# Attention and two feed-forward layers on one core: adjacent heads as pairs, keys on 128 partitions, another order of the first loads

## The chip, the cores and the metric

The kernel runs on one core of a Trainium2 chip. The metric is the device time of one execution in microseconds (us); lower is better. Five engines run side by side: TensorE (PE), VectorE (DVE), ScalarE (ACT), GpSimd (POOL) and SyncE (SP). Each takes its instructions in order. SP only issues DMA transfers; ACT and POOL can issue them too, between their own instructions. SPq, ACTq and POOLq are the places where such an issue shows.

## What is computed

Eight batches of 8 heads, 576 queries, head size 64. Keys and values are first averaged over groups of 8 positions, which leaves 72 of each; the scores, a softmax and the product with the averaged values follow. The result, 4608 rows of 512, passes through two feed-forward layers. The weights are float64 and are turned into float32 in the kernel.

```python
k_p = k.reshape(B, H, 72, 8, D).mean(axis=3)      # v_p likewise
scores = scale * np.matmul(q, k_p.transpose(0, 1, 3, 2))
attn = softmax(scores);  x = matmul(attn, v_p)    # (8, 8, 576, 64) -> (4608, 512)
h = x @ w_in;  x = (h * cos(h)) @ w_out           # 512 -> 2048 -> 512
out = (silu(x @ w_gate) * (x @ w_val)) @ w_out2   # 512 -> 1536 -> 512
```

## The kernel before

**Stages.** First comes an opening part for batch 0 of the attention; then 144 slots, each one 512-row block of tokens times one 128-column block of the first feed-forward layer (9 blocks of rows, 16 of columns); then the second layer. The attention of batches 1 to 7 is spread over the slots, by the tables MID, LATE, EXP and NORM and the first slot of each batch in START (lines 377 to 423).

**Heads.** The 8 heads are worked on as 4 pairs; before, pair p is heads p and p + 4 (`"(r p)"` in the views of q, k and v). The two heads of a pair share the 128 partitions.

**Queries.** `load_q` brings a batch in as four transfers, each of 32 partitions in runs of 32 numbers (128 bytes), so that 32x32 blocks lie ready, and `do_qt` turns each tile of queries with DVE's block transpose. There are five tiles, four of 128 queries and one of 64. `ACT_QUEUE` lists which transfers are issued by ACT: half of batch 0, and all of batches 1 and 3. The others are issued by SP.

**Keys and values.** A raw key tile has 72 partitions, one for each group of 8 positions; three additions (`pool_sum`) sum the 8. Values put the first 64 groups of two heads on 128 partitions, and the last 8 groups of all heads in one more tile. Batch 0 is summed on DVE from `kst` and `vst`, batch 1 on DVE from tiles that borrow the homes of late w_in tiles (`load_kv1`, homes wa3* and wa2*). Batches 2 to 7 are loaded by SP (`load_kv`) and summed on POOL, 8 key tiles and 5 value tiles per batch, one per slot (`do_raw`). `prep_k` turns the sums with TensorE and writes them scaled to `kT`.

**Scores.** `do_s` multiplies, takes the extreme with DVE, and for batches 0 and 1 ACT takes one exponential per head. `do_norm`, `do_pt` and `do_av` follow, and the result goes to `ring`. `x_split` cuts `ring` into a high and a low part, `xhl`.

**Weights.** The 16 tiles of w_in and 16 of w_out, 512 KB each, are turned from float64 by the generator `conv`: on DVE `cv_exp` (L445), `cv_sign` (L456), `cv_high` (L462), `cv_low` (L467) and `cv_mul` (L473), on ACT `cv_bias` (L451); for w_in also a split (L974 on ACT, L987 on DVE). `order` begins with 8 tiles of w_in, and then tiles of w_out and of w_in take turns. `fill(m)` advances the generator by m steps. `load_i(m)` issues the next m loads of w_in, `load_o(m)` those of w_out, which have two buffers. In the first 16 slots there is one `load_i` per slot.

**Order.** The opening part is the string `program`: s, x, p, a are scores, softmax, turn and product of a tile; V, K, U sum values of batch 0, keys and values of batch 1; v and k prepare; f and F advance the conversion; i, o, q load; w makes room for w_out; X is `x_split`. The framework then orders the instructions of each engine by its own planner, so what stands later in the text can be issued earlier.

Of the kernel before, what the change touches and what calls it, by code (L numbers as in the profile page):

```python
# [25 lines left out]
def fused_kernel(  # L26
# [18 lines left out]
    nc = tc.nc  # L45
# [22 lines left out]
    Y32 = NF1  # L68
    ACT_QUEUE = {(0, 0), (3, 1), (1, 1), (3, 0), (1, 0)}

# [12 lines left out]
    ring = const.tile([P, KC, RING], F32, name="ring")  # L83
    xhl = const.tile([P, 2, KC, TB], F32R, name="xhl")

# [66 lines left out]

    kvraw = {}
    kraw1 = []
    vraw1 = []
    pairs = "(r p) (s l) d -> r s p (l d)"
    kview = [k[b].rearrange(pairs, r=2, l=POOL) for b in range(B)]
    vview = [v[b, :, : SM * POOL].rearrange(pairs, r=2, l=POOL) for b in range(B)]
    vleft = [v[b, :, SM * POOL :].rearrange("h (s l) d -> h s (l d)", l=POOL) for b in range(B)]

    def load_kv(b, kind, i):

        rows = SP if kind == "k" else P
        t = kvraw[b, kind, i] = p1a.tile([P, POOL * D], F32, name=f"{kind}raw_{b}_{i}", tag="kv", bufs=2)[:rows]
        if kind == "k":
            nc.sync.dma_start(t, kview[b][i % 2, :, i // 2])
        else:
            for r in range(2):
                nc.sync.dma_start(t[r * SM : (r + 1) * SM], vview[b][r, :, i] if i < NP else vleft[b])

    def load_kv1():

        for p in range(NP):
            t = wts.tile([P, 2, TB], F32, name=f"k1_{p}", tag=f"wa3{p}")
            nc.sync.dma_start(t[:SP], kview[1][:, :, p].rearrange("r s x -> s r x"))
            kraw1.append(t[:SP])
# [20 lines left out]
    def new_kp(b):  # L197
        kps[b] = p1a.tile([SP, NP, 2, D], F32, name=f"kp_{b}", tag="kp")

# [3 lines left out]
    def sum_kv(b, kind, i):  # L203
        if i == 0:
            (new_kp if kind == "k" else new_vp)(b)
        dst = kps[b][:, i // 2, i % 2] if kind == "k" else vps[b][:, i]
        pool_sum(nc.gpsimd, dst, kvraw.pop((b, kind, i)))

    def prep_k(b):

        kp = kps.pop(b)
        ps = psum.tile([P, NP, SP], F32, name=f"kps_{b}", tag="att", bufs=2)
        for p in range(NP):
            nc.tensor.transpose(ps[:, p], kp[:, p].rearrange("s r d -> s (r d)"), ident[:SP, :SP])
        nc.scalar.mul(kT[0:64, :, 0:SP], ps[0:64], -EXP_SCALE)
        nc.scalar.mul(kT[64:128, :, SP:], ps[64:128], -EXP_SCALE)

    def prep_v(b):
        vmh, vml, vl1, vl2 = (av_tile(nm, b) for nm in ("vmh", "vml", "vl1", "vl2"))
        vp = vps.pop(b)  # L220
        if b < ACTB:
            for r in range(2):
                rows, cols = slice(r * SM, (r + 1) * SM), slice(r * D, (r + 1) * D)
                nc.scalar.mul(vmh[rows, :, cols], vp[rows, :NP], 1.0 / POOL)
            nc.vector.tensor_mul(
                vl1[:SM].rearrange("q p (r d) -> q r p d", r=2),
                vp[:SM, NP : NP + 1].rearrange("q (a o) d -> q a o d", a=1).to_broadcast([SM, 2, NP, D]),
                mask[:SM].rearrange("q (r p o) -> q r p o", r=2, o=1).to_broadcast([SM, 2, NP, D]),
            )
            return  # L230
# [10 lines left out]
        )  # L241
        t = t.rearrange("q (r p) d -> q r p d", r=2)
        h2 = vl1.rearrange("q p (r d) -> q r p d", r=2)
# [47 lines left out]
    def do_norm(b, t, pm=None):  # L291
# [16 lines left out]
        for g in range(2):  # L308
            left = pm[:n, H * SM + g * SM : H * SM + (g + 1) * SM].rearrange("q (r p s) -> q p r s", r=2, p=NP)
            if g == 0:  # L310
                nc.vector.tensor_mul(
                    left,
                    e[:, :, SM:].rearrange("q (p r) s -> q p r s", r=2),
                    sm.rearrange("q (p r) o -> q p r o", r=2).to_broadcast([n, NP, 2, SL]),
                )
            elif b >= ACTB:
                nc.vector.tensor_copy(pm[:n, H * SM + SM :], pm[:n, H * SM : H * SM + SM])
# [48 lines left out]

    raws = [(b, kind, i) for b in range(2, B) for kind, m in (("k", H), ("v", NP + 1)) for i in range(m)]

    def do_raw(b, i):
        at = (b - 2) * (H + NP + 1) + i  # L370
        if at + 1 < len(raws):
            load_kv(*raws[at + 1])
        sum_kv(*raws[at])
# [43 lines left out]
    for b in range(1, B):  # L417
        for table, plan in ((exps, EXP), (mids, MID), (lates, LATE), (norms, NORM)):
            for o, x in plan.items():
                at(table, START[b] + o - (b == 1 and x[0] == 'v'), run_item, b, x)  # L420
        if b + 1 < B:
            for i in range(H + NP + 1):
                at(lates, START[b] + i + (b == 1), do_raw, b + 1, i)
# [8 lines left out]
    def cv_load(key, src, home=None):  # L432
        st = raw_tile(f"st_{key}") if home is None else wts.tile([P, 2, TB], F32, name=f"st_{key}", tag=home)
        st = st.rearrange("p a t -> p (a t)")
        src = src if isinstance(src, list) else [src]
        m = P // len(src)
        for i, x in enumerate(src):
            nc.sync.dma_start(st[i * m : (i + 1) * m].bitcast(U64), x)
        cv[key] = st.rearrange("p (t two) -> p t two", two=2)
# [44 lines left out]


    def x_split(half):
        for c in range(KC):
            src = ring[:, c, half * TB : (half + 1) * TB]
            split(xhl[:, 0, c], xhl[:, 1, c], src)

# [10 lines left out]
    def pe_h(s):  # L501
# [3 lines left out]
        for c in range(KC):  # L505
            whi, wlo = wa[j, c][:, 0, o : o + P], wa[j, c][:, 1, o : o + P]
            nc.tensor.matmul(ps, whi, xhl[:, 0, c], start=c == 0, stop=False)  # L507
            nc.tensor.matmul(ps, whi, xhl[:, 1, c], start=False, stop=False)  # L508
            nc.tensor.matmul(ps, wlo, xhl[:, 0, c], start=False, stop=c == KC - 1)  # L509
        hps[s] = ps  # L510
# [121 lines left out]
    def t_steps(q):  # L632
# [4 lines left out]
        for prod, raw, minuend in (  # L637
# [6 lines left out]
            if prod in ("P3", "P4"):  # L644
                o = 2 * (prod == "P4")
                T[prod] = xhl[:, :, o : o + 2]
            else:
# [179 lines left out]
    def out_steps(q):  # L827
# [3 lines left out]
        own = pools2["a"].tile([P, 2, 2, TB], F32R, name=f"op_{q}", tag="tP7")  # L831
        homes = [own, xhl[:, :, 0:2], xhl[:, :, 2:4]]
        b11, b12, b21, b22 = ((e, h) for e in range(2) for h in range(2))
# [172 lines left out]
    vst = p1w.tile([P, 8, TB], F32, name="vst", tag="big1", bufs=1)  # L1006
    kst4 = kst[:SP].rearrange("s (p r) x -> s r p x", r=2)
    load_i(1)
    for r in range(2):
        nc.sync.dma_start(kst4[:, r], kview[0][r])  # L1010
    load_i(1)
    fill(2)
    load_q(0)
    load_i(1)
# [5 lines left out]
    new_kp(0)  # L1020
    for r in range(2):
        pool_sum(nc.vector, kps[0][:, :, r], kst4[:, r])
    prep_k(0)
# [22 lines left out]
    def sum_k1(p):  # L1046
        if p == 0:
            new_kp(1)
        pool_sum(nc.vector, kps[1][:, p], kraw1[p])

    def sum_v1():
# [206 lines left out]
```

## Time and profile before

| | |
|---|---|
| median of 3 runs | 1803.17 us (1802.95 to 1803.2) |
| the profiled execution's own time | 1804.83 us |
| its span in the profile | 1803.1 us |
| PE busy | 1737.5 us (96%) |
| DVE busy | 1263.8 us (70%) |
| ACT busy | 1066.6 us (59%) |
| POOL busy | 171.7 us (10%) |

Times in the profile are microseconds from the start of the span unless marked ns. A busy PE is not PE at its peak, since matmuls are pipelined. An entry such as "[2.40 <-DVE wo L473]" means that the engine sat idle for 2.40 us before this instruction, and that the instruction of line 473 on DVE ended that.

### The profile page before, as it was taken

To read this page: it belongs to the slowest core of one execution; us is meant where nothing else is said; L and a number is where in the kernel's file an instruction comes from. 1 tells how busy PE (TensorE), PEld (TensorE's weight loads), DVE (VectorE), ACT (ScalarE), POOL (GpSimd) and SP (SyncE) were. 2 spreads that over 40 slices of the span, in tenths; PEclk is the share of its full clock that TensorE was granted. 3 is DMA by queue.
4 is the path that set the end of the run, shared out by engine and by line. 5 is a ranking of instruction groups with operands and counts; after the bars stand their busy time and mean duration, and the time that the engine had idled before them with its cause. 6 is when DMAs were issued, how large, how long until landed. Compare 5 with 4: busy or idle time off the path is not lost.

```text
span 1803.1 us, 23421 instructions
## 1 busy us (share of the span) xinstructions
PE 1737.5 (96%) x8044; PEld 1439.4 (80%) x8044; DVE 1263.8 (70%) x2152; ACT 1066.6 (59%) x1933; POOL 171.7 (10%) x254
## 2 busy tenths in 40 slices
PE   2879999999999999999999999999999999999998
PEld 2546587888878888878877888888888888999998
DVE  6898688877877677787875586863584367358446
ACT  3578587777777767778776565533443344344333
POOL 0150513304104022000000000000000000000000
PEclk9989999999999999999999999999999999999999
DMA  9934246446566455474885488576667556787773
GB/s 186 203 104 120 79 165 188 156 131 197 148 205 218 114 198 144 158 220 153 235 275 176 159 320 291 193 252 225 194 200 267 193 192 221 290 265 246 294 249 93
DMA packets 248157, 357.01 MB, mean 198 GB/s; under 512 B 149608, under 2 KB 155752, under 8 KB 248040
## 3 DMA queue, kind: packets, MB, share of 16 engines
q1 hardware_dynamic: 224840, 352.58, 61.7%
q10 hardware_dynamic: 23200, 2.95, 1.1%
q8 instruction: 64, 1.05, 0.2%
q14 instruction: 53, 0.43, 0.1%
HBM read 285.74 MB, written 69.73 MB: 197 GB/s over the span
## 4 chain that ended last, share of the span: by engine, by line
PE 68%; DVE 14%; DMA 9%; ACT 5%; issue 2%; SPq 1%; POOL 0%; ACTq 0%; DVEq 0%
PE X L762 13%; PE oX L892 8%; PE Y L762 7%; PE h L507 4%; PE h L509 4%; PE h L508 4%; PE acc L578 4%; PE oY L892 4%; PE acc L579 4%; PE acc L577 4%; PE Z L762 3%; DMA w2r<-w_dram 2%; PE oZ L892 2%; PE av L358 2%; PE acc L570 2%
## 5 line engine op out<-in xcount | busy, mean ns | idle before, releaser
L762 PE MATMUL X<-t_P,wc 128*128 128x512 f32 (+1 forms) x1080 | 232.6, 367 | 1.0 <-ACT u L811 1.0
L507 PE MATMUL h<-xhl,wa 128*128 128x512 f32 x576 | 231.5, 402 | 0.0
L508 PE MATMUL h<-xhl,wa 128*128 128x512 f32 x576 | 226.3, 393 | 1.3 <-DVE xhl L131 1.3
L509 PE MATMUL h<-xhl,wa 128*128 128x512 f32 x576 | 225.6, 392 | 0.0
L762 PEld LDWEIGHTS X<-t_P,wc 128*128 128x128 f32 x1080 | 196.5, 188 | 27.5 <-ACT u L811 2.4
L578 PE MATMUL acc<-gl,wo_ring 128*128 128x512 f32 x448 | 176.4, 394 | 1.7 <-DVE gl L558 1.5
L577 PE MATMUL acc<-gh,wo_ring 128*128 128x512 f32 x448 | 175.1, 401 | 3.1 <-ACT gh L555 2.9
L579 PE MATMUL acc<-gh,wo_ring 128*128 128x512 f32 x448 | 175.4, 391 | 0.0
L544 DVE SCALAR_TENSOR_TENSOR w<-w,hs 128x512 f32<-128x512 f32 x144 | 102.3, 710 | 49.7 <-ACT w L541 48.4
L516 ACT ACTIVATE hs<-h 128x512 f32<-128x512 f32 x144 | 85.7, 595 | 76.4 <-DVE w L544 47.8
L540 ACT ACTIVATE w<-w 128x512 f32<-128x512 f32 x144 | 91.0, 632 | 64.9 <-DVE w L519 63.8
L507 PEld LDWEIGHTS h<-xhl,wa 128*128 128x128 f32 x576 | 108.7, 189 | 25.7 <-issue 4.1
L508 PEld LDWEIGHTS h<-xhl,wa 128*128 128x128 f32 x576 | 108.7, 189 | 25.3 <-issue 2.4
L509 PEld LDWEIGHTS h<-xhl,wa 128*128 128x128 f32 x576 | 108.5, 188 | 23.8 <-issue 0.9
L519 DVE SCALAR_TENSOR_TENSOR w<-w,hs 128x512 f32<-128x512 f32 x144 | 105.3, 731 | 23.7 <-ACT w L518 23.5
L814 DVE TENSOR_TENSOR p<-p,X 128x512 f32<-128x512 f32 (+1 forms) x60 | 37.9, 632 | 117.0 <-PE X L762 109.5
L558 DVE TENSOR_TENSOR gl<-w,gh 128x512 fp32r<-128x512 f32 x128 | 90.9, 710 | 40.2 <-ACT gh L555 38.6
L130 ACT CAST xhl<-pst 128x1024 fp32r<-128x1024 f32 (+1 forms) x70 | 67.7, 967 | 71.3 <-PE oX L892 26.1
L518 ACT ACTIVATE w<-hs,few 128x512 f32<-128x512 f32 x144 | 104.5, 725 | 7.3 <-DMA w_dram<-ce_w 4.2
L892 PE MATMUL oX<-xhl,wc 128*128 128x512 f32 (+1 forms) x480 | 102.8, 368 | 0.0
L578 PEld LDWEIGHTS acc<-gl,wo_ring 128*128 128x128 f32 x448 | 84.6, 189 | 21.5 <-DVE gl L558 5.2
L577 PEld LDWEIGHTS acc<-gh,wo_ring 128*128 128x128 f32 x448 | 84.1, 189 | 21.7 <-ACT gh L555 4.9
(197 smaller groups left out, 3586.3 us busy)
## 6 DMA issues: line engine op xcount, KB each, us to landing
wc<-wc_dram SPq DMA_DIRECT2D x273, 512.0 KB
wo_ring<-wo_dram SPq DMA_DIRECT2D x112, 512.0 KB
wc_dram<-wc SPq DMA_DIRECT2D x42, 512.0 KB
wc_dram<-ow SPq DMA_DIRECT2D x42, 256.0 KB
y_dram<-yo SPq DMA_DIRECT2D x18, 512.0 KB
w_dram<-ce_w SPq DMA_DIRECT2D x36, 256.0 KB
st_i<-in_moe_w_in_dram SPq DMA_DIRECT2D x32, 256.0 KB
st_o<-in_moe_w_out_dram SPq DMA_DIRECT2D x16, 512.0 KB
```

What stands on the lines that cost most here:

```text
L507: nc.tensor.matmul(ps, whi, xhl[:, 0, c], start=c == 0, stop=False)
L508: nc.tensor.matmul(ps, whi, xhl[:, 1, c], start=False, stop=False)
L509: nc.tensor.matmul(ps, wlo, xhl[:, 0, c], start=False, stop=c == KC - 1)
L518: nc.scalar.activation(w, h, AF.Identity, bias=magic)
L519: nc.vector.scalar_tensor_tensor(out=w, in0=w, scalar=MAGIC, in1=h, op0=ALU.subtract, op1=ALU.subtract)
L540: nc.scalar.activation(w, w, AF.Sin, scale=PI)
L544: nc.vector.scalar_tensor_tensor(out=w, in0=w, scalar=1.0, in1=h, op0=ALU.subtract, op1=ALU.mult, reverse0=True)
L577: nc.tensor.matmul(acc[n][i], a[:, cols], xh, start=f == 0, stop=False)
L578: nc.tensor.matmul(acc[n][i], a[:, cols], xl, start=False, stop=False)
L579: nc.tensor.matmul(acc[n][i], b[:, cols], xh, start=False, stop=f == NF1 - 1)
L762: nc.tensor.matmul(ps[:, :hb], w, t[:, x, c, :hb], start=first and c == 0 and n == 0, stop=c == 1 and n == 2, skip_group_check=not first,)
L892: nc.tensor.matmul(banks[key][m][:, :hb], u, x[:, b, i, :hb], start=first_ and j == i == k == 0, stop=j == NJ - 1 and i == 1 and k == 2, s ...
```

## The change

Pairs become adjacent heads, 2p and 2p + 1, so that the rows of a w_in tile are contiguous and its load is one transfer instead of two. Raw keys get the layout of the values: two heads' first 64 groups on 128 partitions (4 tiles of this kind, NP), and the last 8 groups of the heads in two tiles of 32 partitions, 6 tiles (NK) instead of 8. The keys and values of batches 2 to 7 are loaded from POOL's queue instead of SP's. The queries of batch 0 come in as they lie, five transfers from ACT's queue in runs of 64 numbers (256 bytes), and TensorE turns them, with ACT copying the result; the tile for them shares its place with `xhl`. The queries of the other batches still come in for DVE's transpose, now as 16 transfers per batch, all issued by SP. In the opening part, the sums of batch 1 stand ahead of `x_split`, and all eleven w_in tiles that are still to be loaded (i11) stand ahead of the first two of w_out (o2).

```diff
-    ACT_QUEUE = {(0, 0), (3, 1), (1, 1), (3, 0), (1, 0)}
...
-    qview = q.rearrange("b (r p) (t i) d -> b r i p t d", r=2, i=32)
+    qview = q.rearrange("b (p r) (t i) d -> b r i p t d", r=2, i=32)
...
-                (nc.scalar if (b, r) in ACT_QUEUE else nc.sync).dma_start(
-                    qi[a : a + 32].rearrange("i p (t d) -> i (p t) d", d=32),
-                    qview[b, r, :, :, :, 32 * e : 32 * e + 32].rearrange("i p t d -> i (p t) d"),
-                )
+                for p in range(NP):
+                    nc.sync.dma_start(
+                        qi[a : a + 32, p].rearrange("i (t d) -> i t d", d=32), qview[b, r, :, p, :, 32 * e : 32 * e + 32]
+                    )
...
+    q0 = const.tile([P, 2, KC, TB], F32, name="q0", tag="xhl").rearrange("p a c t -> p (a c) t")
+
+    def load_q0():
+        for t, (t0, n) in enumerate(TILES):
+            nc.scalar.dma_start(
+                q0[:n, t].rearrange("s (h d) -> s h d", h=H), q[0, :, t0 : t0 + n].rearrange("h s d -> s h d")
+            )
...
+    NK = NP + 2
+    kview = [k[b, :, : SM * POOL].rearrange("(g x r) (s l) d -> g x s r (l d)", x=2, r=2, l=POOL) for b in range(B)]
+    kleft = [k[b, :, SM * POOL :].rearrange("(p r) (s l) d -> r s p (l d)", r=2, l=POOL) for b in range(B)]
...
-        if kind == "k":
-            nc.sync.dma_start(t, kview[b][i % 2, :, i // 2])
+        if kind == "k" and i >= NP:
+            nc.gpsimd.dma_start(t, kleft[b][i - NP])
+        elif kind == "k":
+            for x in range(2):
+                nc.gpsimd.dma_start(t[x * SM : (x + 1) * SM], kview[b][i // 2, x, :, i % 2])
         else:
             for r in range(2):
-                nc.sync.dma_start(t[r * SM : (r + 1) * SM], vview[b][r, :, i] if i < NP else vleft[b])
+                nc.gpsimd.dma_start(t[r * SM : (r + 1) * SM], vview[b][r, :, i] if i < NP else vleft[b])
...
-        for p in range(NP):
-            nc.tensor.transpose(ps[:, p], kp[:, p].rearrange("s r d -> s (r d)"), ident[:SP, :SP])
-        nc.scalar.mul(kT[0:64, :, 0:SP], ps[0:64], -EXP_SCALE)
-        nc.scalar.mul(kT[64:128, :, SP:], ps[64:128], -EXP_SCALE)
+        for g in range(2):
+            nc.tensor.transpose(ps[:, g * P : (g + 1) * P], kp[:, 2 * g : 2 * g + 2].rearrange("s r d -> s (r d)"), ident)
+        m = SL * NP
+        nc.tensor.transpose(ps[:, 2 * P :], kp[:m, NP:].rearrange("s r d -> s (r d)"), ident[:m, :m])
+        for r in range(2):
+            rows = slice(r * D, (r + 1) * D)
+            to = kT[rows, :, r * SP : (r + 1) * SP]
+            nc.scalar.mul(to[:, :, :SM], ps[rows, : 2 * P].rearrange("d (p s) -> d p s", p=NP), -EXP_SCALE)
+            nc.scalar.mul(to[:, :, SM:], ps[rows, 2 * P :].rearrange("d (s p) -> d p s", p=NP), -EXP_SCALE)
...
+        if b == 0:
+            ps = psum.tile([P, NP, n], F32, name=f"qp_{t}", tag="hg", bufs=2)
+            for p in range(NP):
+                nc.tensor.transpose(ps[:, p], q0[:n, t, p * P : (p + 1) * P], ident[:n, :n])
+            nc.scalar.copy(qT, ps)
+            return
         nc.vector.transpose(qT, qt_in[b][:, :, t0 : t0 + n])
...
-                src = [w_in[(r * NP + c) * D : (r * NP + c + 1) * D, j * TB : (j + 1) * TB] for r in range(2)]
-                cv_load(keys[u], src, f"wa{j}{c}")
+                cv_load(keys[u], w_in[c * P : (c + 1) * P, j * TB : (j + 1) * TB], f"wa{j}{c}")
...
-        "s0 s1 f4 x0 s2 p0 V0 v x1 p1 f3 s3 a0 x2 p2 f3 x3 i1 p3 a1 w F3 X s4 i1 q o2 "
-        "K0 K1 K2 K3 U0 x4 k b i3 f6 "
+        "s0 s1 f4 x0 s2 p0 V0 v x1 p1 f6 s3 F3 a0 x2 p2 x3 p3 a1 w K0 K1 K2 U0 X s4 q i11 o2 "
+        "x4 k b f6 "
```

## Rows read from the trace of the kernel before

**Rows 1.** The page: busy us and share of the span of each engine.
```profile
PE 1737.5 (96%) x8044; PEld 1439.4 (80%) x8044; DVE 1263.8 (70%) x2152; ACT 1066.6 (59%) x1933; POOL 171.7 (10%) x254
```

**Rows 2.** Stretches: length, busy time of each engine, clock, DMA share, GB/s.
```profile
0.00:72.00 72.00, 35.87 (x93) 20.71 (x93) 48.73 (x103) 30.57 (x105) 5.97 (x21) 1.00 0.97 196
72.00:140.00 68.00, 56.68 (x201) 35.53 (x201) 67.09 (x113) 49.48 (x130) 31.84 (x41) 0.92 0.48 127
140.00:200.00 60.00, 59.80 (x218) 36.21 (x217) 44.65 (x86) 47.90 (x112) 5.76 (x9) 1.00 0.34 91
```

**Rows 3.** The chain that ended last, 0 to 160 us: start, length, what.
```profile
5.91 11.02 SPq L148
...
47.95 9.49 DMA qi<-in_q_dram
57.46 0.32 ACTq L148
...
63.74 8.69 DMA st_i<-in_moe_w_in_dram
...
72.52 0.43 DVE wo L445
...
139.15 1.98 PE acc L570 x4
```

**Rows 4.** What DVE waited for, 0 to 140 us: total, times, longest.
```profile
DVE ce_i L445 <- DMA st_i<-in_moe_w_in_dram: 7.1, 1, 7.1
...
DVE kst L190 <- DMA kst<-in_k_dram: 3.9, 1, 3.9
DVE ce_i L456 <- ACT ce_i L451: 3.2, 3, 2.0
DVE wo L445 <- DMA st_i<-in_moe_w_in_dram: 2.1, 2, 1.7
```

**Rows 5.** DVE's groups by shape, 0 to 72 us: count, busy us, mean ns.
```profile
L257 DVE STREAM_TRANSPOSE qT<-qi 128x512 f32<-128x512 f32 x4 | 2.8, 703 | 0.0
...
L190 DVE TENSOR_TENSOR k<-k 72x512 f32<-72x512 f32 x4 | 2.6, 671 | 0.0
L190 DVE TENSOR_TENSOR kst<-kst 72x1024 f32<-72x1024 f32 x2 | 2.4, 1222 | 3.9 <-DMA kst<-in_k_dram 3.9
L190 DVE TENSOR_TENSOR k<-k 72x256 f32<-72x256 f32 x4 | 1.6, 416 | 0.0
...
L192 DVE TENSOR_TENSOR kp<-k 72x128 f32<-72x128 f32 x4 | 1.0, 271 | 0.0
...
L257 DVE STREAM_TRANSPOSE qT<-qi 128x256 f32<-128x256 f32 x1 | 0.4, 433 | 0.0
```

**Rows 6.** The same view and one form: 72 to 140 us, then 140 to 200 us.
```profile
L544 DVE SCALAR_TENSOR_TENSOR w<-w,hs 128x512 f32<-128x512 f32 x6 | 5.4, 903 | 0.0
...
L544 DVE SCALAR_TENSOR_TENSOR w<-w,hs 128x512 f32<-128x512 f32 x9 | 6.2, 688 | 4.8 <-ACT w L541 4.8
```

**Rows 7.** Four instructions of ACT, PE and DVE in order of time: start, length.
```profile
36.93 0.58 ACT L328 COPY pth<-pt 128x512 f32<-128x512 f32 x1
...
39.61 1.08 PE L326 MATMUL pt<-ident,vst 128*128 128x128 f32 x4 [2.20 <-DVE vst L304]
...
64.66 0.43 DVE L445 TENSOR_SCALAR wo<-st_o 128x512 uint32<-128x512 uint32 x1 [0.53 <-DMA st_o<-in_moe_w_out_dram]
...
89.97 1.02 PE L570 MATMUL acc<-w,wo 128*128 128x512 f32 x2
```

**Rows 8.** DMA issues of SP in order of time: start, time in issue, count.
```profile
162.27 4.40 SPq L148 DMA_DIRECT2D qi<-in_q_dram  x3
```

**Rows 9.** POOL's last key sum of batch 2, and its use on PE.
```profile
106.56 0.65 POOL L192 TENSOR_TENSOR kp<-kraw 72x64 f32<-72x64 f32 x1
...
178.61 0.42 PE L214 MATMUL kps<-ident,kp 72*128 72x72 f32 x4
```

**Rows 10.** What PE waited for, 300 to 835 us, the longest entry.
```profile
PE acc L578 <- DVE gl L558: 3.5, 5, 1.5
```

More of the change, by code (lines that the diff above doesn't have):

```diff
@@ L83, in fused_kernel @@
     ring = const.tile([P, KC, RING], F32, name="ring")
-    xhl = const.tile([P, 2, KC, TB], F32R, name="xhl")
     mask = few[:, 0]
@@ L197, in new_kp @@
     def new_kp(b):
-        kps[b] = p1a.tile([SP, NP, 2, D], F32, name=f"kp_{b}", tag="kp")
+        kps[b] = p1a.tile([P, NK, D], F32, name=f"kp_{b}", tag="kp")
     def new_vp(b):
@@ L205, in sum_kv @@
             (new_kp if kind == "k" else new_vp)(b)
-        dst = kps[b][:, i // 2, i % 2] if kind == "k" else vps[b][:, i]
+        dst = vps[b][:, i] if kind == "v" else kps[b][:, i] if i < NP else kps[b][: SL * NP, i]
         pool_sum(nc.gpsimd, dst, kvraw.pop((b, kind, i)))
@@ L211, in prep_k @@
         kp = kps.pop(b)
[L212 to L216 removed]
+        ps = psum.tile([P, NP * SP], F32, name=f"kps_{b}", tag="att", bufs=2)
+        for g in range(2):
+            nc.tensor.transpose(ps[:, g * P : (g + 1) * P], kp[:, 2 * g : 2 * g + 2].rearrange("s r d -> s (r d)"), ident)
+        m = SL * NP
+        nc.tensor.transpose(ps[:, 2 * P :], kp[:m, NP:].rearrange("s r d -> s (r d)"), ident[:m, :m])
+        for r in range(2):
+            rows = slice(r * D, (r + 1) * D)
+            to = kT[rows, :, r * SP : (r + 1) * SP]
+            nc.scalar.mul(to[:, :, :SM], ps[rows, : 2 * P].rearrange("d (p s) -> d p s", p=NP), -EXP_SCALE)
+            nc.scalar.mul(to[:, :, SM:], ps[rows, 2 * P :].rearrange("d (s p) -> d p s", p=NP), -EXP_SCALE)
     def prep_v(b):
@@ L365, in do_av @@
             done += m
-    raws = [(b, kind, i) for b in range(2, B) for kind, m in (("k", H), ("v", NP + 1)) for i in range(m)]
+    raws = [(b, kind, i) for b in range(2, B) for kind, m in (("k", NK), ("v", NP + 1)) for i in range(m)]
     def do_raw(b, i):
-        at = (b - 2) * (H + NP + 1) + i
+        at = (b - 2) * (NK + NP + 1) + i
         if at + 1 < len(raws):
@@ L421, in fused_kernel @@
         if b + 1 < B:
-            for i in range(H + NP + 1):
+            for i in range(NK + NP + 1):
                 at(lates, START[b] + i + (b == 1), do_raw, b + 1, i)
@@ L434, in cv_load @@
         st = st.rearrange("p a t -> p (a t)")
[L435 to L438, printed above, removed]
+        nc.sync.dma_start(st.bitcast(U64), src)
         cv[key] = st.rearrange("p (t two) -> p t two", two=2)
@@ L483, in chain_tile @@
         return chain.tile([P, TB], dtype, name=nm, tag=tag, bufs=bufs)
+    xhl = []
     def x_split(half):
+        if not xhl:
+            xhl.append(const.tile([P, 2, KC, TB], F32R, name="xhl", tag="xhl"))
         for c in range(KC):
             src = ring[:, c, half * TB : (half + 1) * TB]
-            split(xhl[:, 0, c], xhl[:, 1, c], src)
+            split(xhl[0][:, 0, c], xhl[0][:, 1, c], src)
     wa = {}
@@ L831, in out_steps @@
         own = pools2["a"].tile([P, 2, 2, TB], F32R, name=f"op_{q}", tag="tP7")
-        homes = [own, xhl[:, :, 0:2], xhl[:, :, 2:4]]
+        homes = [own, xhl[0][:, :, 0:2], xhl[0][:, :, 2:4]]
         b11, b12, b21, b22 = ((e, h) for e in range(2) for h in range(2))
@@ L1006, in fused_kernel @@
     vst = p1w.tile([P, 8, TB], F32, name="vst", tag="big1", bufs=1)
-    kst4 = kst[:SP].rearrange("s (p r) x -> s r p x", r=2)
     load_i(1)
+    for g in range(2):
+        for x in range(2):
+            nc.sync.dma_start(kst[x * SM : (x + 1) * SM, 2 * g : 2 * g + 2], kview[0][g, x])
     for r in range(2):
-        nc.sync.dma_start(kst4[:, r], kview[0][r])
+        nc.sync.dma_start(kst[: SL * NP, NP + r], kleft[0][r])
     load_i(1)
     fill(2)
-    load_q(0)
+    load_q0()
     load_i(1)
@@ L1020, in fused_kernel @@
     new_kp(0)
-    for r in range(2):
-        pool_sum(nc.vector, kps[0][:, :, r], kst4[:, r])
+    for g in range(2):
+        pool_sum(nc.vector, kps[0][:, 2 * g : 2 * g + 2], kst[:, 2 * g : 2 * g + 2])
+    pool_sum(nc.vector, kps[0][: SL * NP, NP:], kst[: SL * NP, NP:NK])
     prep_k(0)
@@ L1048, in sum_k1 @@
             new_kp(1)
-        pool_sum(nc.vector, kps[1][:, p], kraw1[p])
+        pool_sum(nc.vector, kps[1][:, 2 * p : 2 * p + 2] if p < 2 else kps[1][: SL * NP, NP:], kraw1[p])
     def sum_v1():
```

37 lines of the change are left out of this document (18 added, 19 removed).

## The prediction

> **What bounds the kernel now.** The page comes first: PE is busy for 96% of the span [rows 1], so only a shorter wait, or less work on the engine that PE waits for, can move the end. The view by stretches says where PE isn't full: 35.87 of the first 72 us and 56.68 of the next 68, against 59.80 of 60 from 140 to 200 us [rows 2]. From 300 to 835 us the longest entry of what PE waited for is 3.5 us in all, and it is DVE arithmetic, not a load [rows 10]. So the case is decided in the first 140 us.
>
> There the chain that ended last is to be read with the stretches. Up to 72.5 us it is made of loads and of queues: SP stuck for 11.02 us in one issue of batch 0's queries, then ACT kept by the queries of batch 1 for 9.49 us up to its own issue at 57.46, then 8.69 us for a tile of w_in, for which the conversion on DVE (L445) waits until 72.52 [rows 3]. From there DVE is busy 67.09 of 68 us [rows 2], and the chain comes to PE at 139.15 [rows 3]. After that PE is full. So I take the date at which DVE has its work of the first 140 us done as the quantity that moves; what is won there is given to the end one for one, since nothing later waits for what this change touches. DVE is busy 48.73 + 67.09 = 115.8 us of 140 and idle 24.2 [rows 2].
>
> **The change part by part, in us off DVE's date.**
>
> *Queries of batch 0 turned by TensorE.* DVE loses five block transposes, 4 at 0.703 and one at 0.433: -3.2 [rows 5]. PE gains 20 turns, 4 to a tile, 1.08 by the nearest row, and ACT a copy out of PSUM of 0.58 for each tile [rows 7]. Neither engine is full here (PE 35.87, ACT 30.57 of 72 [rows 2]); the turns can run ahead, and the copy stands where DVE's 0.70 stood. Cost nothing; without that cover 5 x (1.08 + 0.58) = 8.3, the upper bound.
>
> *Keys on 128 partitions.* A key group of two heads costs 0.671 + 0.416 + 0.271 = 1.36 on DVE [rows 5]. Batch 1 had four such sums and gets three: -1.4. Batch 0 had two of twice the width, 1.222 + 0.671 + 0.416 = 2.31 each, and gets three of 1.36: -0.5. `prep_k` issues 3 turns for 4 on PE and 4 scalings for 2 on ACT; per batch that is a few tenths off the path.
>
> *Fewer key tiles on POOL.* While POOL is busy (31.84 of 68 us [rows 2]) the same DVE instruction takes 903 ns instead of 688 [rows 6]. A batch has 11 tiles instead of 13. If all 113 instructions of DVE lost 0.215, that would be 24, and 2/13 of it 3.7; the lower bound is 0. I take -1.0, since most forms are shorter or have one input.
>
> *The queues.* SP no longer stands 11.02 in the queries of batch 0; ACT issues these, ahead of the work that needs it. ACT isn't held by batch 1's queries any more: DVE's 2.0 wait for L451 is the end of that hold [rows 4]. All w_in tiles are loaded ahead of w_out, one issue each: the 2.1 that DVE waited for w_in in its second stretch can go [rows 4]. Against this, batch 1's queries are now 16 issues on SP in front of the eleven w_in tiles. The nearest row is batch 2: three of its four transfers held SP for 4.40 [rows 8], so about 5.9 for a batch of the same bytes, or up to 22 if all stand as the first batch's did [rows 3]. I take 5.9, as the queues are no longer full of another 2 x 11 us of the same kind; DVE has w_in 0 to 4, both batches' sums and batch 0's softmax to do meanwhile. Of the idle 24.2, the first 7.1 and the 3.9 for the first keys stay [rows 4]; at most 13.2 can go, at least 0. I take -3.0, the 2.0 and half of the 2.1.
>
> *Moved past a queue.* The first w_out tile is in DVE's hands at 64.66 now [rows 7]. After the change it stands behind six loads of 1.18 MB (k, q, v of two batches) and 16 of 0.524 MB; with its own that is 16.0 MB, and at 196 GB/s [rows 2] it lands at about 82. PE uses it at 89.97 now [rows 7], some 9 earlier in this forecast, 81; its conversion takes some 4 (five DVE instructions of 0.4 to 0.7). So PE's first use comes 4 to 5 late, in a stretch where PE has 68 - 56.68 = 11.3 idle [rows 2] and DVE has w_in to convert. I cost it at 0; the bound is in the rivals.
>
> *Loads from POOL.* They are issued between POOL's sums. Batch 2's last key sum ends at 107.2, PE wants it at 178.61 [rows 9]: 71 of cover. The price of a load's issue on POOL is in no row; 12 key loads would have to take 6 each to eat it. Cost nothing.
>
> *Later batches.* Six times 16 query issues instead of 4, the same bytes and run lengths, in stretches in which no load ends a wait of PE [rows 10]. Nothing; at most the SP time of 12 more issues, which reaches PE only through a late weight.
>
> The sum: 3.2 + 1.4 + 0.5 + 1.0 + 3.0 = 9.1 less. Against the profiled execution's 1804.83 that is 1795.7; the median of the runs is 1803.17, 1.66 below that execution, so 1794 for a median.
>
> Of the key loads the rows show only that DVE waited 3.9 for the first [rows 4]. The Trainium skill (DMA: Bandwidth & Descriptors, "Why a DMA increments its semaphore by 16 and not by 1") says that a transfer runs on the largest number of engines up to 16 that divides its slowest dimension, thus 12 for 72 partitions and 16 for 64. By that, as an estimate, the 2.36 MB of keys of batches 0 and 1 would take 12 us instead of 16 if nothing else filled the idle engines, and the sum would be 13 less; no row here tells the engines apart.
>
> **The rivals.**
>
> *A larger gain.* Softmax of batch 0 starts earlier and w_in is there before DVE wants it, so that most of the 13.2 goes: 6.1 + 10 = 16, 1787. For it speaks that every wait in the chain before 72.5 is a load or a queue [rows 3]; against it, that DVE's order is fixed and its head can wait while other work stands ready.
>
> *Only the work goes.* Idle time moves but doesn't shrink: 3.2 + 1.4 + 0.5 + 1.0 = 6.1 less, 1797.
>
> *No change.* Late w_in and w_out eat what the DVE work gives: if DVE stands for 6 to 12 at the head of its queue, the time is 1800 to 1806. DVE already waits for such heads [rows 4].
>
> *Slower: w_out late.* DVE meets the first w_out step (L445) where it does now, at 64.66, and it lands at 82: 17.4 idle, and only 9.1 won, so 8 more: 1811. It decides from 9 us of idle at that head on. For it: the order of the conversion is the same in the text, only the loads are moved. Against it: the planner that orders the instructions knows the loads' order, and PE uses that tile only 25 us after DVE has it [rows 7].
>
> *POOL's loads starve.* With DVE full from 72 to 140, POOL's sums already stretch, and its issues might too; if each key load took 6 or more, PE would wait for `kps` at slot 12, 12 x (price - 6) on the end; at 8 each, 24 more: 1818. The Trainium skill (SBUF — State Buffer, "SBUF: two separate sides") speaks against the change here: for a transfer issued by GpSimd the descriptors can't be written while DVE holds the port that the two share, so that it waits for DVE. By that rule this rival is the mechanism; no row of before has a load from POOL.
>
> **How the numbers follow.** About 0.2% (3.6 us) is what a measurement tells from no change, so "same" is 1799.6 to 1806.8. The forecast, 7 to 13 less: 0.44. Larger gain: 0.17. Only the work (1797 to 1799.5): 0.11. No change: 0.13. W_out late: 0.11. POOL: 0.04. Faster 0.72, same 0.13, slower 0.15. The likeliest is 1794, its own range 1790 to 1796. For 8 in 10 the range takes in the smaller gain and no change above, to 1806, and half of the larger gain below, to 1783; some 0.05 lie below it and 0.15 above.
>
> **What would show it.** Right: DVE's 128x512 block transposes before 72 us gone; no ACT wait behind a query issue near 48 to 58; DVE's busy time of the first 140 us down by about 6; the chain's step from DVE to PE near 130 instead of 139.15; equal PE work from there. Wrong: a wait of DVE's L445 for w_out, or PE's first `acc` (L570) standing at w_out's conversion, later than 89.97; PE waiting at `kps`; weights late behind 16 query issues in a later batch; or a first `h` on PE that isn't earlier although DVE is, which would make PE's own chain of batch 0 the bound.

## The result, and the profile after

The changed kernel takes 1815.52 us (median of 4 runs, 1812.84 to 1817.11) and the kernel before 1803.18 beside it: a ratio of 1.0062 [1.0048, 1.0076]. The forecast was 1794 in a range of 1783 to 1806, with a chance of 0.15 for slower. The profiled execution has a span of 1813.1 us, 10.0 more than before.

First the engines' busy time on the page, then the stretches of [rows 2].

```profile
PE 1746.9 (96%) x8056; PEld 1445.1 (80%) x8056; DVE 1259.5 (69%) x2147; ACT 1075.9 (59%) x1956; POOL 195.0 (11%) x338
```

```profile
0.00:72.00 72.00, 47.74 (x136) 29.45 (x137) 43.14 (x95) 33.52 (x122) 10.99 (x30) 1.00 0.92 228
72.00:140.00 68.00, 48.20 (x166) 31.05 (x165) 63.74 (x112) 52.31 (x124) 30.10 (x51) 0.82 0.28 90
140.00:200.00 60.00, 60.00 (x220) 36.83 (x219) 44.43 (x86) 46.54 (x110) 14.64 (x26) 1.00 0.40 110
```

DVE's busy time up to 140 us fell from 115.8 [rows 2] to 43.14 + 63.74 = 106.9. Part of that is work that went and part is work not yet done: DVE has 207 instructions in these two stretches where it had 216, and the change takes only five away (x2152 [rows 1] to x2147). And PE is busy for only 48.20 of the second stretch (before 56.68), at a mean granted clock of 0.82 (before 0.92): it did more up to 72 us and less behind. What DVE waited for up to 140 us answers [rows 4]:

```profile
DVE xhl L129 <- ACT xhl L128: 11.4, 3, 8.9
DVE ce_i L466 <- DMA st_i<-in_moe_w_in_dram: 6.4, 2, 5.8
DVE mx L301 <- PE s L297: 5.7, 6, 1.7
DVE kst L207 <- DMA kst<-in_k_dram: 3.7, 1, 3.7
...
DVE ce_i L477 <- ACT ce_i L472: 0.8, 1, 0.8
```

The first line is new: 11.4 us at the low part of the first `x_split`. SP's issues at that time (start, time in issue, count):

```profile
38.52 15.80 SPq L147 DMA_DIRECT2D qi<-in_q_dram  x16
54.36 10.40 SPq L459 DMA_DIRECT2D st_i<-in_moe_w_in_dram  x9
```

Batch 1's 16 query transfers hold SP for 15.80 us, and the nine w_in tiles come after them. That looks like the reason why DVE had no conversion to do meanwhile; a run below shows that it isn't. Where the end was lost is seen in the date of the first `h` matmul of a slot, minus that of the kernel before (worked out from the traces; the last two rows are runs told below):

```
slot                                      0     4      8     24     48     64    108    end of span
changed kernel                          -5.4  -0.8   +3.0   +3.2   +7.2  +11.9   +9.0   +10.0
changed, keys and values from SP        -7.0  -8.7   -0.2   +0.2   -0.6   -0.7   -3.1    -2.6
changed, GpSimd's loads, one buffer     -6.6  -6.2   -1.1   -3.2   -4.1   -3.8   -6.0    -4.2
```

The first `h` is 5.4 us earlier, nearly all of that is gone by slot 4, and a second loss comes long after the opening, between slots 24 and 64.

### The profile page after: what moved, and what is told of

Same layout as the page of the kernel before. It is cut to its first block, busy times and chain, and to the rows that moved or that the text cites. A ratio compares the mean times of both kernels' runs of the same rounds, so it can differ in the third digit from the quotient of the medians.

```text
span 1813.1 us, 23507 instructions
## 1 busy us (share of the span) xinstructions
PE 1746.9 (96%) x8056; PEld 1445.1 (80%) x8056; DVE 1259.5 (69%) x2147; ACT 1075.9 (59%) x1956; POOL 195.0 (11%) x338
## 4 chain that ended last, share of the span: by engine, by line
PE 78%; DVE 11%; DMA 5%; ACT 4%; issue 1%; SPq 0%; ACTq 0%; DVEq 0%
PE X L787 14%; PE oX L917 8%; PE Y L787 7%; PE h L532 5%; PE h L533 5%; PE h L534 5%; PE acc L603 5%; PE acc L602 5%; PE acc L604 5%; PE oY L917 4%; PE Z L787 4%; PE av L382 3%; PE acc L595 2%; PE s L297 2%; PE oZ L917 2%
## 5 line engine op out<-in xcount | busy, mean ns | idle before, releaser
L569 DVE SCALAR_TENSOR_TENSOR w<-w,hs 128x512 f32<-128x512 f32 x144 | 103.5, 718 | 48.8 <-ACT w L566 47.5
```

Source lines behind the costliest of these rows:

```text
L569: nc.vector.scalar_tensor_tensor(out=w, in0=w, scalar=1.0, in1=h, op0=ALU.subtract, op1=ALU.mult, reverse0=True)
```

## The experiments

Theory A: the loss is from loading later keys and values from GpSimd's queue. Rival B: it is from the opening (w_in behind the queries, DVE at the first `x_split`). Rival C: it is from the 16 query issues per batch on SP. The times of all runs, each beside the kernel before on the same chip:

```
run                          us        range                ratio to before, 95% interval
e1_kv_from_SP                1802.56   1801.49 to 1805.22   0.9987 [0.9977, 0.9997]
e2_before_kv_from_POOL       1820.76   1818.31 to 1824.58   1.0090 [1.0072, 1.0109]
e4_w_in_ahead_of_q1          1820.98   1817.54 to 1822.04   1.0086 [1.0071, 1.0101]
e6_w_in_ahead_of_kv1         1815.01   1811.76 to 1823.32   1.0064 [1.0041, 1.0087]
e7_conv_ahead_of_split       1812.32   1810.64 to 1812.56   1.0040 [1.0027, 1.0054]
e9_short_sums_POOL           1791.97   1788.51 to 1793.23   0.9927 [0.9912, 0.9942]
e10_short_sums_SP            1792.84   1792.25 to 1794.15   0.9936 [0.9922, 0.9949]
e11_sum_ahead_of_load        1813.46   1810.94 to 1815.65   1.0049 [1.0034, 1.0063]
f1_one_kv_buffer             1800.74   1798.27 to 1805.07   0.9977 [0.9965, 0.9989]
f2_kv_from_ACT               1847.79   1843.79 to 1851.07   1.0232 [1.0208, 1.0257]
f3_batch2_from_SP            1810.40   1807.68 to 1813.77   1.0027 [1.0017, 1.0037]
f4_batch2_from_POOL          1805.48   1803.75 to 1809.31   1.0003 [0.9993, 1.0014]
g4_before_POOL_one_buffer    1800.85   1798.91 to 1803.24   0.9980 [0.9970, 0.9991]
g5_SP_one_buffer             1823.97   1821.64 to 1829.96   1.0116 [1.0094, 1.0138]
g1_one_buffer_w_in_early     1801.01   1797.02 to 1805.13   0.9976 [0.9965, 0.9988]
g2_one_buffer_w_out_early    1801.16   1797.31 to 1807.16   0.9980 [0.9965, 0.9995]
```

The kernel before took 1803.18 us beside the changed kernel and 1804.95 to 1805.74 in the other groups, so a difference between times of two groups can be off by up to 2.6 us; the ratios are taken within a group.

### Which part costs it

**The loads back to SP.** In `load_kv`, three times:

```diff
-            nc.gpsimd.dma_start(t, kleft[b][i - NP])
+            nc.sync.dma_start(t, kleft[b][i - NP])
```

> The changed kernel, with the keys and values of batches 2 to 7 loaded from SP's queue again; all else stays. Theory A (the loads from POOL's own queue run ahead, so that POOL's sums of a batch run back to back in one cluster, and DVE, slowed all through it, is late for PE): the loss of slots 24 to 64 (9 us by the starts of the slots) goes, 1804 to 1808. Theory B (the opening alone is worse, since DVE stands at x_split while w_in waits behind the queries): no change, 1813 to 1817. Rival C (the slots lose by the 16 query issues per batch on SP): no gain, or 2 to 4 us slower, since SP has more to issue.

**Only GpSimd's loads,** put into the kernel before (the same edit the other way round):

> The kernel before, with this one part of the change: keys and values of batches 2 to 7 loaded from POOL's queue, 8 key tiles of 72 partitions as before. Theory A: slower by 7 to 10 us, 1810 to 1813, lost between slots 24 and 64, with POOL's sums in clusters of 12 us and more. Theory B: 1803, or 1 to 3 less, since SP is free of waits behind POOL's sums. Rival C: 1803.

**The opening's order,** first w_in ahead of batch 1's queries, then three w_in tiles ahead of batch 1's keys and values:

```diff
-        "... U0 X s4 q i11 o2 "
+        "... U0 X s4 i11 q o2 "
```

> The changed kernel with the eleven w_in loads ahead of batch 1's queries in SP's queue (i11 q instead of q i11). Theory B: DVE's idle time of 50 to 58 us and at w_in goes in part, the opening gains 3 to 6 us at slot 20, 1809 to 1812; the losses of slots 24 to 64 stay. Theory A alone: the opening stays, 1815. If batch 1's queries are then late, PE waits for the first scores of batch 1 and it is 2 to 5 slower.

```diff
+    load_i(3)
     load_kv1()
-    load_i(1)
...
-        "... U0 X s4 q i11 o2 "
+        "... U0 X s4 q i9 o2 "
```

> The changed kernel with three w_in loads ahead of batch 1's keys and values (instead of one behind them), nine left for later. The planner then sees w_in early and puts conversion steps on DVE ahead of the low part of x_split. Theory B: DVE's wait of 8.88 us for x_split is filled with conversion, the opening gains 5 to 9 us, 1806 to 1811. Theory A alone: nothing, 1815.

The first two settle it: without GpSimd's loads the changed kernel is 13.0 us faster (1815.52 to 1802.56), and these loads alone cost the kernel before 15.6 (1805.15 in that group to 1820.76), more than the 7 to 10 that was expected. C falls with the first: all query issues stay, and the loss is gone. B gets no support: with both orders w_in is issued sooner, slot 0 begins 5.1 and 9.4 us before that of the kernel before, and slot 8 13.1 and 2.7 after it (5.4 before and 3.0 after in the changed kernel). The first order is no clean test of B, since batch 1's queries then come late; what PE waited for from 60 to 165 us:

```profile
PE s L297 <- DVE qT L285: 16.3, 2, 13.0
```

### How a load costs it

GpSimd's groups in the changed kernel (count, busy us, mean ns, idle before):

```profile
L181 POOL DMA_DIRECT2D vraw<-in_v_dram x60 | 32.6, 548 | 7.4 <-POOL vp L209 3.8 <-POOL kp L209 3.5
L207 POOL TENSOR_TENSOR vraw<-vraw 128x256 f32<-128x256 f32 x30 | 25.9, 864 | 17.4 <-DMA vraw<-in_v_dram 17.2
L178 POOL DMA_DIRECT2D kraw<-in_k_dram x48 | 25.5, 537 | 3.0 <-POOL vp L209 3.0
```

An issue takes GpSimd some 0.54 us, and the largest sums of values wait 17.2 us for their loads in all. Two suspects, then: the issues, or the sums that they let run in one row. Two of the three adds of each sum were left out, with either queue (the outputs are those of other keys and values):

```diff
-        pool_sum(nc.gpsimd, dst, kvraw.pop((b, kind, i)))
+        raw = kvraw.pop((b, kind, i))
+        nc.gpsimd.tensor_add(dst, raw[..., :D], raw[..., D : 2 * D])
```

> The changed kernel (loads on GpSimd's queue) with two of the three adds of each sum of later keys and values on GpSimd left out (the outputs are those of other keys and values); GpSimd keeps its 120 transfer instructions. Theory A1 (the sums, run in one row, slow DVE; the transfer instructions are harmless): without most of the sums nothing is left to slow DVE, and this run and the same cut with the loads on SP agree within 3 us, both 1790 to 1800. Rival A2 (the transfer instructions themselves, some 0.55 us each on GpSimd, slow DVE): this run stays 10 to 13 us over the other.

> The run with the loads on SP, with the same two of three adds left out (outputs of other keys and values). Theory A1: 1790 to 1800, as the run with the loads on GpSimd. Rival A2: 1790 to 1800 while the run with the loads on GpSimd is at 1802 to 1812. If sums spaced by SP's queue cost DVE nothing, this run is at 1801 to 1803, as with all the adds.

1791.97 and 1792.84: with one add in three left, the queue makes no difference, so the 120 issues cost nothing that can be measured, and it is the sums that cost. Even with SP's loads the adds left out were worth 9.7 us (1802.56 to 1792.84). The trace of the changed kernel says the same of single instructions (worked out from it, 60 to 700 us): DVE's SCALAR_TENSOR_TENSOR of 128x512 took 684 ns on average beside nothing of GpSimd, 686 beside an issue alone and 894 beside adds alone. What a sum does to DVE is seen in the same forms of the changed kernel, first 84 to 106 us, with GpSimd busy, then 112 to 145, with GpSimd idle:

```profile
L483 DVE TENSOR_SCALAR st_i<-st_i 128x512 uint32<-128x512 uint32 x3 | 2.5, 849 | 0.0
L494 DVE SCALAR_TENSOR_TENSOR wo<-st_i,wo 128x512 f32<-128x512 f32 x2 | 2.4, 1209 | 0.0
L569 DVE SCALAR_TENSOR_TENSOR w<-w,hs 128x512 f32<-128x512 f32 x2 | 2.3, 1142 | 0.0
```

```profile
L569 DVE SCALAR_TENSOR_TENSOR w<-w,hs 128x512 f32<-128x512 f32 x5 | 3.4, 682 | 0.0
...
L494 DVE SCALAR_TENSOR_TENSOR wo<-st_i,wo 128x512 f32<-128x512 f32 x4 | 2.7, 672 | 0.0
...
L483 DVE TENSOR_SCALAR st_o<-st_o 128x512 uint32<-128x512 uint32 x6 | 2.5, 412 | 0.0
```

0.67 us becomes 1.1 to 1.2. The Trainium skill (SBUF — State Buffer, "SBUF: two separate sides") says that a GpSimd instruction and a DVE instruction that needs the port pair they share shut each other out for a whole instruction; two inputs from SBUF are enough, against a GpSimd instruction that reads SBUF. The direction agrees with the rows of L494 and L569, which have two inputs; L483 has one and went from 0.41 to 0.85 us. No run here shows the port itself.

The stretch 84 to 106 us of the changed kernel, then of the run with SP's loads:

```profile
84.00:106.00 22.00, 7.43 (x28) 5.94 (x28) 21.59 (x32) 15.24 (x35) 18.91 (x32) 0.66 0.25 72
```

```profile
84.00:106.00 22.00, 11.41 (x36) 7.80 (x37) 22.00 (x46) 21.52 (x46) 0.65 (x1) 0.73 0.09 27
```

DVE is full in both, and gets 32 instructions done in the one, 46 in the other. GpSimd is busy for 18.91 us in the one (12.33 of adds and 6.58 of issues, worked out from the trace) and for 0.65 in the other. SP's own issues in that run say what keeps GpSimd away:

```profile
65.30 16.21 SPq L178 DMA_DIRECT2D kraw<-in_k_dram  x7
102.93 1.90 SPq L459 DMA_DIRECT2D st_o<-in_moe_w_out_dram  x2
104.87 0.47 SPq L178 DMA_DIRECT2D kraw<-in_k_dram  x1
```

From 81.5 to 102.9 SP's head is a w_out load that waits for a buffer which DVE's conversion (L494) has to free, and the keys stand behind it. So in this run SP's queue kept the sums out of the stretch; GpSimd's own queue doesn't hold them. The kernel before, with SP's queue as well, had its sums there all the same:

```profile
84.00:106.00 22.00, 18.12 (x71) 11.79 (x69) 21.61 (x34) 17.24 (x42) 15.96 (x20) 0.92 0.56 134
```

This stretch shows what adds do to DVE; it isn't where the changed kernel loses against the kernel before.

**Sum ahead of load.** The load of the next tile was put behind the sum:

```diff
-        if at + 1 < len(raws):
-            load_kv(*raws[at + 1])
         sum_kv(*raws[at])
+        if at + 1 < len(raws):
+            load_kv(*raws[at + 1])
```

> The changed kernel with its loads still on GpSimd's queue, but each load issued behind the sum before it instead of ahead of it, so that GpSimd waits for every transfer and its sums don't run in one row. Theory A1: gaps of some 2 us between sums let DVE recover, and most of the loss is gone: 1802 to 1808. Rival A2: the same transfer instructions, the same loss: 1813 to 1818. If the sums come too late for keys' transposes, PE waits at kps in the later batches and it is over 1818.

This told nothing: the planner put GpSimd's instructions into the order they had. Its 1813.46 is close to a repetition of the changed kernel.

**One buffer.** With one raw tile in place of two, a load can't be issued before the last sum is done:

```diff
-        ... tag="kv", bufs=2)[:rows]
+        ... tag="kv", bufs=1)[:rows]
```

> The changed kernel (loads on GpSimd's queue) with one buffer for later keys and values in place of two: GpSimd issues a load, waits for it to land, sums, and issues the next, so that its sums have gaps of some 2 to 3 us. Theory A1 (sums in one close row): DVE recovers in the gaps, 1802 to 1808. Rival A3 (what counts is that the sums fall into the stretches in which DVE is already the last to arrive, 80 to 110 us above all, however close they stand): the first cluster still lies there, 1810 to 1816.

1800.74, 14.8 us faster than the changed kernel and 4.8 faster than the kernel before. GpSimd now waits for its own loads:

```profile
POOL kp L209 <- PE kps L233: 243.2, 6, 62.8
POOL kraw L207 <- DMA kraw<-in_k_dram: 105.0, 36, 6.4
POOL vraw L207 <- DMA vraw<-in_v_dram: 98.8, 30, 5.7
```

And the stretch 84 to 106 us of the same run:

```profile
84.00:106.00 22.00, 10.27 (x32) 7.64 (x32) 22.00 (x40) 19.51 (x39) 12.37 (x19) 0.69 0.10 31
```

The sums still fall into 84 to 106 us, but GpSimd is busy for 12.37 us in place of 18.91 (8.91 of adds in place of 12.33), and DVE does 40 instructions. That speaks for A1 (how close they stand) against A3 (where they fall), and doesn't part them, since fewer adds fall into the stretch too. The edit has a rival of its own: one buffer may do something else. It was tried with GpSimd's loads in the kernel before, and with SP's loads in the changed one:

> The kernel before with later keys and values loaded from GpSimd's queue, and one buffer for them. Theory A1 (the close row of sums was all that the GpSimd loads cost): from 1820.8 with two buffers to 1800 to 1806. Rival: one buffer cures something that only the changed kernel has, and this stays above 1812.

> The changed kernel with the loads on SP, and one buffer. Theory A1: the sums were spaced already; the same time within 3 us as with two buffers, 1800 to 1805. Rival (one buffer helps by itself): under 1799. If a load that waits for its buffer holds w_out's loads back on SP: over 1806.

In the kernel before, one buffer takes GpSimd's loads from 1820.76 to 1800.85, so the cure doesn't hang on the rest of the change. With SP's loads it costs 21.4 us, and the wait that its expectation named last is there. What DVE waited for from 60 to 160 us, its longest line:

```profile
DVE wo L466 <- DMA st_o<-in_moe_w_out_dram: 12.9, 5, 6.4
```

A key load that waits for its only buffer holds up w_out behind it in the same queue. The line accounts for 12.9 of the 21.4 us; the rest was not followed.

What parts A1 from A3 better is DVE's time over the whole span. The kernels of each half of the table have the same adds on GpSimd (234 and 198) and the same DVE instructions. The last column adds up by how much each DVE instruction that overlapped an add was longer than the mean of its shape beside none (worked out from the traces):

```
                                        time, us   DVE busy, us   longer beside adds, us
before                                  1803.18    1263.8         39.8
before, GpSimd's loads                  1820.76    1282.2         59.0
before, GpSimd's loads, one buffer      1800.85    1263.2         41.0
changed kernel                          1815.52    1259.5         42.6
changed, keys and values from SP        1802.56    1248.2         30.2
changed, GpSimd's loads, one buffer     1800.74    1247.5         29.2
```

The same adds in one row lengthen DVE's work by 12 to 19 us more than the same adds with gaps, and the time differs by 13 to 20. So how close they stand counts; that it also counts where they fall is not ruled out, and why a close row is dearer to DVE is not shown.

### Which batches, and another queue

Only batch 2's loads on SP, then only batch 2's on GpSimd (`(nc.sync if b == 2 else nc.gpsimd).dma_start`, and the reverse), then all on ScalarE (`nc.scalar.dma_start`):

> The changed kernel with only batch 2's keys and values back on SP's queue; batches 3 to 7 stay on GpSimd's. Slot 8 should begin where it does with all loads on SP (147.4 us, 3.2 us earlier than in the changed kernel) and the losses from slot 28 on stay: 1810 to 1813. If the loss is all in the opening and what follows from it, 1802 to 1805.

> The mirror of the run before: only batch 2's keys and values from GpSimd's queue, batches 3 to 7 from SP's. Slot 8 at 150 to 151 us as in the changed kernel, nothing lost after that: 1804 to 1807. If the loss is all in the opening, 1813 to 1816.

> The changed kernel with the loads of later keys and values on ScalarE's queue: they are issued only as ScalarE's own work advances, and w_out's loads on SP no longer stand ahead of them or behind them. Theories A1 and A3: the sums are spread as ScalarE reaches the loads, 1800 to 1807, with ScalarE some 120 instructions longer. If a load that waits for its buffer holds up ScalarE's copies, PE waits for ScalarE and it is over 1815.

Over the run with all loads on SP, batch 2 alone costs 2.9 us (1805.48) and batches 3 to 7 cost 7.8 (1810.40): 10.7 of the 13.0, mostly behind the opening. The rest lies within the runs' spread of some 2 to 6 us, and so does batch 2's 2.9 nearly (the intervals of the ratios overlap). ScalarE's queue is worst, 45 us: what PE waited for over the whole span shows, among others,

```profile
PE s L297 <- DVE qT L285: 20.1, 1, 20.1
PE h L532 <- ACT hs L541: 18.9, 8, 7.7
```

The loads stand among ScalarE's copies. ScalarE's own order from 82 us on shows them holding it up:

```profile
82.44 12.14 ACTq L181 DMA_DIRECT2D vraw<-in_v_dram  x10
94.86 5.96 ACTq L178 DMA_DIRECT2D kraw<-in_k_dram  x4
100.87 0.72 ACT L543 ACTIVATE w<-hs,few 128x512 f32<-128x512 f32 x1 [19.76 <-DMA st_i<-in_moe_w_in_dram]
```

ScalarE does no work for 19.76 us while 14 loads go out from its queue one by one. The profile puts that wait down to a w_in tile; but the last of the loads in front of the instruction ends at 100.82, just before it starts.

A later place where GpSimd's row hits, in the changed kernel:

```profile
528.00:532.00 4.00, 2.71 (x12) 1.90 (x11) 3.93 (x7) 3.96 (x8) 2.26 (x5) 1.00 0.73 248
532.00:536.00 4.00, 1.89 (x4) 1.34 (x5) 4.00 (x5) 2.18 (x5) 3.54 (x6) 0.63 0.76 143
536.00:540.00 4.00, 4.00 (x11) 3.07 (x10) 2.44 (x4) 1.51 (x3) 3.06 (x6) 0.51 0.96 243
540.00:544.00 4.00, 4.00 (x20) 3.29 (x19) 0.45 (x2) 1.32 (x2) 3.26 (x7) 1.00 0.80 261
```

PE is idle for 1.3 and 2.1 us while DVE is full with 7 and 5 instructions. Then PE has work, but at 0.51 of the clock (1.2 GHz): 11 matmuls in 4 us, where the next 4 us hold 20 at full clock. So PE pays for its wait twice. Between the first `h` of slots 24 and 64 the changed kernel takes 272.7 us, with PE idle for 8.2 and a mean granted clock of 0.988 (3.2 us of clock time); with SP's loads it takes 263.2, with 3.2 idle at 1.00, and with one buffer 263.5, with 2.6 idle at 1.00 (worked out from the traces). These 9 us are the larger part of the 12.5 between the spans of the changed kernel and the run with SP's loads.

### Why the opening's gain is so small

Conversion steps ahead of `x_split`, with SP's loads:

```diff
-        "... U0 X s4 q i11 o2 "
-        "x4 k b f6 "
+        "... U0 f8 X s4 q i11 o2 "
+        "x4 k b "
```

> The changed kernel with later keys and values back on SP's queue, and with 8 steps of w_in's conversion put ahead of the first x_split in DVE's order (they stood behind it). Theory C: the work taken out of the opening bought little because DVE stands at x_split's low part for 8.9 us (50 to 60 us) and the conversions behind it are late for h at 80 to 100 us; with conversion ahead of it DVE is busy there, slots 4 to 8 begin 5 to 8 us earlier than in the run with the loads on SP alone, and the time is 1794 to 1799. Rival D: at 50 to 60 us the w_in tiles have not landed (w_in stands behind 16 query transfers on SP), so DVE waits for the transfer in place of x_split and x_split comes later as well: 1801 to 1805, slot 8 where it was.

Then, on the run with one buffer, three w_in loads ahead of batch 1's keys (the edit shown above), and only four w_in loads ahead of w_out (`i4` for `i11`):

> The run with GpSimd's loads and one buffer, and three of w_in's loads ahead of batch 1's keys and values (9 in place of 11 behind the queries). Theory: VectorE's 8.9 us at the first x_split are filled with conversions, slot 8 begins 4 to 8 us earlier, 1793 to 1797. Rival: what VectorE does earlier it does not do earlier in sum, since the planner's order and the transfers' sum hold, and slot 8 stays within 2 us: 1799 to 1803.

> The run with GpSimd's loads and one buffer, and four w_in loads ahead of the two of w_out in place of eleven. If w_out behind all of w_in is late for the first accumulations (2.6 us longest wait there): 1796 to 1799. If the order is harmless, as the prediction had it: 1799 to 1803. If w_in is then late for h: over 1804.

The first missed by far. The planner kept the steps where they were: the timeline has DVE's wait of 8.88 us for the low part at 56.61, and the first of the steps at 59.52, behind it. Slot 4 began 16.9 us earlier than before and slot 8 10.2 later. The other two change nothing (1801.01 and 1801.16 against 1800.74), w_out behind eleven w_in tiles costs nothing that can be measured, and w_in sooner gains nothing. A slot's date alone doesn't tell the end: with four w_in loads ahead, slot 8 begins 13.1 us before that of the kernel before, and at slot 12 4.2 of it are left.

That w_in stands behind batch 1's queries is not why DVE stands at `x_split` either. With w_in ahead of the queries (e4) its loads go out from 35.79 on, the fourth and the sixth of them have landed at 49.07 and 54.09, and DVE stands there as long:

```profile
35.79 29.53 SPq L459 DMA_DIRECT2D st_i<-in_moe_w_in_dram  x12
...
58.63 0.69 DVE L129 TENSOR_TENSOR xhl<-ring,xhl 128x512 fp32r<-128x512 f32 x1 [8.89 <-ACT xhl L128]
```

It is DVE's order that puts the conversions behind it. DVE's account up to the first `h` of slot 8 (worked out from the traces) says what happened:

```
kernel                                 slot 8 begins   DVE busy   DVE idle
before                                     147.6         122.8      24.8
before, GpSimd's loads, one buffer         147.6         118.5      29.2
changed, keys and values from SP           147.4         113.8      33.6
changed, GpSimd's loads, one buffer        146.5         114.3      32.2
changed, the same, w_in early              145.0         112.3      32.7
```

From before to the changed kernel with SP's loads, 9.0 us of DVE's busy time are gone and 8.8 us of idle time have come. The longest new wait is the one at `x_split` (8.9, 11.4 with the two after it), and there DVE waits for PE, which is at batch 0's products. The place that `xhl` shares with batch 0's queries isn't what it waits for: ACT copies the last of them at 40.12. The chain that ended last, in the changed kernel:

```profile
41.93 9.24 PE av L382 x16
...
54.79 9.27 PE av L382 x16
64.06 2.11 PE s L297 x8
66.17 0.73 PE h L532
```

The products of batch 0 (L382) run on PE up to 64.06, and `h` follows them. How much of PE's time up to there is the queries' turns was not tried by itself.

That the rest of the change is worth nothing that can be measured follows from two runs of equal time: one buffer and GpSimd's loads give 1800.85 in the kernel before and 1800.74 in the changed one (ratios 0.9980 and 0.9977). The first moves only the queue and the buffer.

## Why the prediction was wrong, point by point

- **The failed step: "Loads from POOL ... Cost nothing."** It priced only lateness, and there it was right: PE's waits at `kps` are for DVE's sums of the opening, none for a sum of GpSimd's. It didn't price what the sums do to DVE once SP's queue no longer spaces them: 13.0 us of time, with 12.4 us more of lengthened DVE instructions (42.6 against 30.2). The rows were at hand: 903 against 688 ns [rows 6]. They were used for the number of tiles, not for their spacing.
- **The rival "POOL's loads starve"** had the place and not the mechanism. An issue took 0.54 us with DVE full, and a load landed 3.0 (keys) and 3.2 us (values) after its issue at the median. The rule of the Trainium skill that it cited (SBUF — State Buffer, "SBUF: two separate sides"), by which the descriptors wait for DVE, showed here in no wait of PE; the other half of that section, a DVE instruction shut out by GpSimd's, was passed over.
- **"Nothing later waits for what this change touches"** failed with it: of the 10.0 us in the span, 3.0 were there at slot 8, the others came behind it. A sign that it named for being right even came, the chain's step from DVE to PE, at 112.89 in place of 139.15, and the end is later all the same: the date of DVE's work in the opening doesn't carry to the end one for one.
- **Queries, keys and fewer key tiles: -6.1 of DVE work.** Right in kind, and rather more: 9.0 less up to slot 8 with SP's loads. The first two terms came as forecast (worked out from that run's trace): five block transposes gone for 3.2 us, batch 1's key sums from 5.43 to 4.09, batch 0's from 4.63 to 4.15. What fewer key tiles gave by themselves was not tried.
- **Queues: -3.0 of idle time.** Wrong in sign: +8.8. The waits that it named did go: DVE waits 0.8 us for ACT's step of the conversion where it waited 3.2, and no longer 2.1 for w_in tiles at the `wo` steps. What it left out is the new wait of 11.4 at `x_split`. Batch 1's queries held SP for 15.80 us and not 5.9, and the upper bound of 22 was nearer, but that isn't the cause. DVE, said to have enough to do meanwhile, had its conversions behind `x_split` in its order and stood there. PE's own chain of batch 0, named last as what would make the forecast wrong, sets that date, though the first `h` did come 5.4 us earlier.
- **W_out late: 0.** Right in price: no wait for a w_out transfer in the changed kernel, and the earlier w_out made no difference. But the sign named for being wrong came, far beyond the 4 to 5 us: DVE takes the first w_out tile at 105.33 (64.66 before), with no wait for its transfer, and PE's first `acc` stands at w_out's conversion at 112.89 (89.97 before). With w_out's loads ahead it begins at 95.62, and the time is the same.

```profile
105.33 0.55 DVE L466 TENSOR_SCALAR wo<-st_o 128x512 uint32<-128x512 uint32 x1
...
112.89 3.49 PE L595 MATMUL acc<-w,wo 128*128 128x512 f32 x4 [2.52 <-DVE wo L494]
```

- **Only the work, 1797; no change, 1800 to 1806:** without GpSimd's loads the time is 1802.56, a gain of 2.6 against the group's 1805.15, ratio 0.9987, less than the 3.6 us that the prediction set as the least that can be told from no change.

## What to carry to other kernels

A queue is also a brake. Before transfers are moved to a queue of their own, ask what work they release, when that work will now run, and whom it slows there; being early is not free when the work that it releases slows the engine that is the bound. And work taken off an engine can be worth nothing if it next stands at a wait: find the instruction behind it in its order, and what that one waits for. Fewer buffers can be the better setting, by the queue that they are loaded from: here one in place of two took 14.8 us off with GpSimd's loads and cost 21.4 with SP's.

## What the runs showed of the hardware

- DVE instructions of 128x512 that take 0.67 to 0.68 us beside an idle GpSimd took 1.1 to 1.2 us on average beside a busy one, and a form with one input went from 0.41 to 0.85. Beside an issue of GpSimd's alone the form with two inputs took 686 ns, beside nothing of GpSimd's 684.
- GpSimd's own issue of a transfer took 0.54 us, and 120 of them (with 12 smaller key loads among them) cost the kernel nothing that can be measured.
- The same 198 adds on GpSimd lengthened DVE's instructions by 42.6 us when they ran in close rows and by 29.2 to 30.2 with gaps between them (234 adds: 59.0 against 39.8 to 41.0).
- In the 8 us up to 536 PE was idle for 3.4; its granted clock was then 0.51 (1.2 GHz) for 4 us, though PE was busy for all of them.
